# Memory attention feeding a channel mix: nine tokens a partition in head halves, 32x64 tiles for values and token mix, mu by small matmuls, steps placed anew

## The chip, the cores and the metric

One Trainium2 chip, one of its cores. The time is the device time in microseconds of one execution. The kernel before took 222.5 us (median of 9 runs, 221.21 to 223.9); the profiled execution is one of these. A core has a matrix engine (TensorE, PE in the profile; PEld is its weight load), VectorE (DVE), ScalarE (ACT), GpSimd (POOL) and SyncE (SP). Here POOL issues most loads, SP the stores.

## What is computed

q, k, v are (8, 8, 576, 64), phi is (8, 8, 576, 32): batch, head, token, width. All inputs and the output are fp32.

```
a = exp(phi - max); a = a / (sum over the 576 tokens + 1e-9)
k_m, v_m = a^T k, a^T v                     # 32 memory slots a head
e = exp(q k_m^T / 8); attn = e / sum(e)     # over the 32 slots
x = attn v_m                                # heads side by side: (8, 576, 512)

x_prev = x one token later, zero at the first
xk = mu_k * x + (1 - mu_k) * x_prev ;  xr likewise with mu_r
out = sigmoid(xr @ w_r) * (relu(xk @ w_k)^2 @ w_v)     # w_k 512x1024, w_v 1024x512, w_r 512x512
```

The kernels leave the subtraction of the maxima out and do the matrix work in bf16 with fp32 sums.

## The kernel before

The 4608 tokens run through two halves. The attention half works batch by batch (8 batches) and leaves xk and xr transposed, features on the partitions, in two rings `xk_T` and `xr_T` of four batches (2304 columns). The channel mix works in 9 chunks of 512 tokens, whatever batch they belong to. Each chunk has 16 pieces: 8 keys (`key`, L523: four matmuls of 512 columns into one PSUM bank, relu on ScalarE, square on VectorE), 4 gates (`gate`, L537: xr @ w_r, exp; log and exp give the sigmoid for two gates at once) and 4 values (`value`, L556: eight matmuls, the product with the gate on VectorE, the store from SP). In the chunks between the first and the last the order is g0 g1 v0 v1 g2 g3 v2 v3 behind the keys.

The order of all engines is written out by hand in `PLAN`, a list of words: `3:s0+av` is step s0 of batch 3 with its PSUM tiles taken from the pools a and v in turn (a: 3 banks, k: 2, v: 3); `c2:10` is piece 10 of chunk 2 (keys take their bank from k, gates and values from v); `busyN` is N idle matmuls of 512 columns. Each word issues its instructions on all engines; an engine then runs its own in this order. The steps of a batch:

- `load` (`reload`): the loads of batch b+2 on POOL, converted to bf16 on the way for q, k and v. With b+2 over 7 it issues nothing. The buffers are two, so a load waits for the last reader of batch b.
- `exp`: exp of phi; `z` (`esum`): its sum over tokens by matmuls with a column of ones, then the reciprocal rz on VectorE.
- `k`, `v`, `kv` (`ekv`, L268): a^T k and a^T v, 32x64 a head; `nk` (L287), `nv` (L298): times rz, for k twice side by side, for v under a mask into a block-diagonal tile `vbd` of two heads.
- `tk` (L309): transpose of k_m. `q0` to `q3` (`tr_q`, L329): transposes of q on TensorE, copied out by VectorE (in batch 0 half of them by ScalarE). `qx` (`cross_q`, L321): the same by a transposing DMA on SP, for batches 6 and 7.
- `s0`, `s1` (`scores`, L346): for four heads (group c) k_m times q, 32x288 a head and half of the tokens; exp on ScalarE (L350) into `e`.
- `l0` to `l3` (`denom`, L360): sums over the slots by a block of ones, log on ScalarE (L362). `h0z` to `h3z` and `r0z`, `r1z` (`recip`, L367): exp of the negative. `y0` to `y3` and `w0`, `w1` (`weigh`, L374): their product with e on VectorE, into `at`.
- batches 2 to 7: `x0` to `x3` (`values`, L387), copied out by ScalarE (L391), `dd` (`diff`, L400) on VectorE, `k0d`, `k2d`, `r0d`, `r2d` (`mix`, L412) on VectorE.
- batches 0 and 1 mix on TensorE: `nkx`, `nrx` (`norm_mu`, L422) put mu and 1 - mu into the values, `mk0` to `mk3` and `mr0` to `mr3` (`mixed`, L444 and L448) multiply them with the tokens and the tokens before, copied out by ScalarE and VectorE (L453). `mub`, `mum0`, `mum1` (L220, L233) spread mu over the slots; `mu` (L226) puts it on the feature partitions.

Tokens are not kept in their order. Of k, v and phi, partition p holds tokens 4p to 4p+3 of the first 512, and the last 64 tokens sit in a fifth slot of 64 partitions. q has six tokens on each of 96 partitions. The columns of xk are grouped by that slot, `JT = (0, 2, 4, 1, 3, 5)`, in two halves of 288, so that the token before is another group of columns; `store` (L504) puts them back.

```
pss = [ps_tile([128, HALF], F32, "nops") ...]          # values(c, hf): one matmul for each pair of heads
matmul(pss[jj], lhsT=vbd[64 rows of pair jj, c], rhs=at[the same rows, c, half hf])
dst = x[:, 2 * c + jj, half hf]
```

Of the kernel before, what the change touches and what calls it, by code (L numbers as in the profile page):

```python
# [18 lines left out]
    "0:exp 0:z 0:mub 0:mum0 0:mum1 0:k 0:nk 0:busy2 0:tk 0:q0+v 0:q1 0:s0+av 0:l1 0:l0 0:q2+v 0:h0z 0:y0 0:h1z 0:y1",  # L19
    "0:q3+k 0:v 7:load 0:nrx 0:s1+ka 0:l2+v 0:h2z 0:busy1 0:nkx 0:y2 0:l3 0:h3z 0:y3 0:mk0+vv 0:mk1+va 0:busy2",  # L20
    "0:busy2 0:mk3+vv 0:mk2+ak c0:0 c0:1 c0:2 c0:3 c0:4 c0:5 0:mr0+aa 0:mr2+vv c0:6 c0:7 0:mr1+va c0:8 0:mr3+av",
    "1:exp c0:9 c0:10 c0:11 0:load 0:busy1 1:z+v 0:busy1 c0:12 1:k 1:nk 1:q0+k 1:q1+v 0:mu 1:q3 1:tk+k 1:s0+kv",
    "1:q2+v 1:v+v 1:s1+kv 1:l0 1:nrx 1:l1 1:h1z 1:y1 c0:13 1:h0z 1:y0 1:nkx 1:l2 2:exp 1:l3+k 1:load 1:h3z 1:h2z",
    "1:y2 c0:14 c0:15 1:y3 2:z 1:mk1+ka 1:mr1+kv 1:mr3+vv 2:q1 1:mk2+va 1:mr2+ak 2:q0+k 1:mk0+va 2:q2+v 2:q3",
    "1:mk3+ka 1:mr0+vk 2:kv 2:nk c1:0 2:tk+v 2:nv c1:1 c1:2 2:s1+av 2:s0+vv c1:3 c1:4 2:load 2:l3 2:l0 2:l1 c1:5",
    "3:exp c1:6 2:l2+v c1:7 c1:8 3:z 2:r1z c1:9 3:q0 3:q1+v 3:q2 2:w1 c1:10 2:x2+ka 2:r0z 2:x3+ka 3:kv+v 3:nk 2:w0",
    "3:nv c1:11 3:q3+k 3:tk 2:x1+aa 2:x0+kv 2:dd 2:k2d c1:12 3:s0+av 3:s1+aa 3:load 2:k0d c1:13 c1:14 3:l0+k 4:exp",
    "2:r2d c1:15 c2:0 3:l3 3:l1+v 3:r0z c2:1 4:q3 3:w0 3:l2+v c2:2 4:q0 4:q2+v 3:r1z c2:3 4:z c2:4 3:w1 4:kv",
    "3:x1+vv 4:nv 3:x0+va c2:5 3:x3+av 2:r0d 4:nk 3:x2+vv 3:dd c2:6 c2:7 c2:8 5:exp 3:k2d 4:q1 c2:9 4:tk+v c2:10",
    "4:load c2:11 4:s1+ak 6:qx 4:s0+va 3:k0d 5:kv 3:r2d 5:z+v 5:q2+k 4:l3 5:nk 4:l2+k 5:nv c2:12 4:r1z 4:w1 c2:13",  # L30
    "c2:14 c2:15 5:q0+v 4:l1 4:l0+k c3:0 5:q1 6:exp c3:1 3:r0d 5:q3+v c3:2 5:load 6:z+v 4:r0z 5:tk+v 4:w0 c3:3 c3:4",
    "c3:5 4:x3+va 5:s0+va 5:s1+va c3:6 c3:7 c3:8 4:x1+av 4:x2+ka 4:x0+av 6:kv+k 6:nv 6:nk 4:dd 4:k2d c3:9 7:exp",
    "c3:10 c3:11 c3:12 4:k0d 5:l1 4:r0d 5:l0+v 5:r0z 5:w0 5:l3+k 5:l2 7:z+k c3:13 c3:14 6:tk+v c3:15 5:r1z 5:w1",
    "c4:0 c4:1 6:s1+aa 6:s0+av c4:2 5:x2+va 6:load 5:x1+av 7:kv 7:nk c4:3 c4:4 7:qx c4:5 c4:6 c4:7 6:l0+v 4:r2d",
    "5:x0+aa 5:x3+kv 5:dd c4:8 c4:9 6:l3 c4:10 c4:11 7:tk 6:l2+k 5:k2d 6:l1 6:r0z 7:nv 5:k0d c4:12 6:w0 7:s0+aa",
    "7:s1+kv c4:13 6:r1z 6:w1 c4:14 c4:15 c5:0 c5:1 c5:2 c5:3 c5:4 c5:5 5:r2d c5:6 6:x2+va 6:x0+aa c5:7 c5:8",
    "6:x1+ak 5:r0d 6:x3+av c5:9 7:l2+k 6:dd c5:10 6:k0d 7:l0 7:l1+k 7:r0z c5:11 c5:12 c5:13 7:w0 6:k2d 7:l3 c5:14",
    "c5:15 7:r1z c6:0 c6:1 c6:2 c6:3 7:w1 6:r0d c6:4 c6:5 c6:6 c6:7 c6:8 c6:9 6:r2d c6:10 7:x1+av 7:x3+kk 7:x2+aa",
    "c6:11 7:x0+kv 7:dd 7:k0d c6:12 7:k2d c6:13 c6:14 c6:15 c7:0 c7:1 c7:2 c7:3 c7:4 c7:5 c7:6 c7:7 c7:8 c7:9 7:r2d",
    "7:r0d c7:10 c7:11 c7:12 c7:13 c7:14 c7:15 c8:0 c8:1 c8:2 c8:3 c8:4 c8:5 c8:6 c8:7 c8:8 c8:9 c8:10 c8:11 c8:12",  # L40
    "c8:13 c8:14 c8:15",
# [8 lines left out]
NQ = 6  # L50
JT = (0, 2, 4, 1, 3, 5)
NB = 4
TAIL = 512
# [3 lines left out]
def kernel(  # L57
# [13 lines left out]
    nc = tc.nc  # L71
# [9 lines left out]
    NT = S - TAIL  # L81
    HALF = S // 2
    QR = S // NQ
# [10 lines left out]

    NJ = NB + 1
    kvs = [const.tile([128, 2, H, NJ, D], BF16, name=f"kv{i}") for i in range(2)]
    qs = [const.tile([QR, H, NQ, D], BF16, name=f"q{i}") for i in range(2)]
    ems = [const.tile([128, NJ, H, M], BF16, name=f"em{i}") for i in range(2)]
# [5 lines left out]

    def load_phi(b, engs):
        phm = ld.tile([128, H, NB, M], F32, name="phm", tag="phm")
        pht = ld.tile([NT, H, M], F32, name="pht", tag="pht")
        n = H // len(engs)
        for i, eng in enumerate(engs):
            h = slice(i * n, (i + 1) * n)  # L110
            eng.dma_start(
                out=phm[:, h].rearrange("p h j m -> p h (j m)"),
                in_=phi[b, h, 0:TAIL, :].rearrange("h (p j) m -> p h (j m)", j=NB))
        engs[0].dma_start(out=pht, in_=phi[b, :, TAIL:S, :].rearrange("h s m -> s h m"))
        loads[b] = {"phm": phm, "pht": pht}

    def load_rows(dst, src, parts=1):
        n = H // parts
        for i in range(parts):
            h = slice(i * n, (i + 1) * n)  # L120
            nc.gpsimd.dma_start(
                out=dst[:, h, 0:NB, :].rearrange("p h j d -> p h (j d)"),
                in_=src[h, 0:TAIL, :].rearrange("h (p j) d -> p h (j d)", j=NB))
            if i == 0:
                nc.gpsimd.dma_start(out=dst[:NT, :, NB, :],
                                    in_=src[:, TAIL:S, :].rearrange("h s d -> s h d"))

    def load_q(b, parts=1):
        n = H // parts
        for i in range(parts):  # L130
            h = slice(i * n, (i + 1) * n)
            nc.gpsimd.dma_start(  # L132
                out=qs[b % 2][:, h].rearrange("p h j d -> p h (j d)"),
                in_=q[b, h].rearrange("h (p j) d -> p h (j d)", j=NQ))

    def load_batch(b):
        for what in LOADS.get(b, LOADS[None]):
            if what == "phi":
                load_phi(b, [nc.gpsimd])
            elif what == "q":  # L140
                load_q(b)
            else:
                load_rows(kvs[b % 2][:, "kv".index(what)], (k, v)["kv".index(what)][b])

    load_phi(0, [nc.sync, nc.scalar])
    load_rows(kvs[0][:, 0], k[0])
    load_q(0, 2)
    make_identity(nc, identity)
    load_rows(kvs[0][:, 1], v[0], 2)
    nc.vector.memset(zeros, 0.0)  # L150
    for i in range(2):
        nc.vector.memset(kvs[i][64:128, :, :, NB, :].rearrange("p a h d -> p (a h) d"), 0.0)
        nc.vector.memset(ems[i][64:128, NB], 0.0)
# [4 lines left out]
    mu_r = const.tile([64, 2, 2, 2 * D], F32, name="mu_r")  # L158
    sel = const.tile([64, 128], F32, name="sel")
    nc.vector.memset(mu_r, 0.0)  # L160
    nc.vector.memset(sel, 0.0)
    for jj in range(2):
        nc.vector.memset(sel[32 * jj:32 * jj + 1, 64 * jj:64 * jj + 64], 1.0)
        for w, mu in enumerate((moe_mu_k, moe_mu_r)):
            nc.sync.dma_start(out=mu_r[32 * jj:32 * jj + 1, w],
                              in_=mu.rearrange("(c j x) -> j c x", c=2, j=2)[jj:jj + 1])
    mu_bs = []
# [11 lines left out]
    for what in ORDER:  # L179
        if what == "wv":  # L180
            nc.gpsimd.dma_start(out=wv_sb, in_=wv_v)
        elif what == "phi":
            load_phi(1, [nc.gpsimd])
        elif what == "q":
            load_q(1)
        else:
            load_rows(kvs[1][:, "kv".index(what)], (k, v)["kv".index(what)][1])
# [4 lines left out]
    ones = const.tile([128, 1], BF16, name="ones")  # L192
    nc.vector.memset(ones, 1.0)

    maskk = const.tile([128, 2, D], BF16, name="maskk")
    sumh = const.tile([128, 4, M], BF16, name="sumh")
    nc.vector.memset(maskk, 0.0)
    nc.vector.memset(sumh, 0.0)
    for g in range(4):
        r = slice(g * M, (g + 1) * M)  # L200
        nc.vector.memset(maskk[r, g % 2, :], 1.0)
        nc.vector.memset(sumh[r, g, :], 1.0)
    mu1 = const.tile([128, 2 * ND], F32, name="mu1")
    mu_m = const.tile([128, 2, 2, 2, 2 * D], F32, name="mu_m")
# [13 lines left out]
    def load_mu_b():  # L218
        ps = psum.tile([128, 2, 2, 2 * D], F32, name="mub", tag="pk", bufs=2)
        nc.tensor.matmul(ps.rearrange("p w c x -> p (w c x)"), lhsT=sel,  # L220
                         rhs=mu_r.rearrange("p w c x -> p (w c x)"), start=True, stop=True)
        mu_bs.append(ps)
# [5 lines left out]

    def spread_mu(w):

        def go():
            mask = maskk.rearrange("p h d -> p (h d)").unsqueeze(1).to_broadcast([128, 2, 2 * D])
            nc.vector.tensor_mul(mu_m[:, w, 0], mask, mu_bs[0][:, w])  # L233
            nc.vector.tensor_sub(mu_m[:, w, 1], mask, mu_m[:, w, 0])
        return go


    def attention(b):
        st = {}

        def ps_tile(shape, dtype, name):
# [4 lines left out]
            return psum.tile(shape, dtype, name=name, tag=tag, bufs={"at": 3, "pk": 2, "pv": 3}[tag])  # L246
        x0 = b * S % RING
        kv5, em = kvs[b % 2], ems[b % 2]

        def exp_phi():  # L250
            L = loads[b]
            nc.scalar.activation(em[:, 0:NB].rearrange("p j h m -> p h j m"), L["phm"], AF.Exp)  # L252
            nc.scalar.activation(em[:NT, NB], L["pht"], AF.Exp)

        def heads(j, lo, n):
# [352 lines left out]
```

## Time and profile before

| | us |
|---|---|
| median of 9 runs | 222.5 |
| the profiled execution | 221.21 |
| its span in the profile | 219.4 |
| keys L523, TensorE busy | 66.9 |
| values of the channel mix L556, TensorE busy | 65.9 |
| gates L537, TensorE busy | 35.1 |
| TensorE, all | 201.2 |
| ScalarE, all | 162.1 |
| VectorE, all | 139.6 |

The busy time of an engine counts instructions that it runs; overlapping matmuls are counted once. Line numbers are those of the kernel before. A timeline row merges neighbouring instructions of one line and gives the start of the first, the length until the last ends, and how many they are; since matmuls overlap at their ends, the distance to the next row's start is a better measure of what a row costs. A bracket at a row's end tells how long the engine stood idle ahead of it and what released it. TensorE's granted clock is given as full throughout.

### The profile page before, as it was taken

To read this page: it belongs to the slowest core of one execution; us is meant where nothing else is said; L and a number is where in the kernel's file an instruction comes from. 1 tells how busy PE (TensorE), PEld (TensorE's weight loads), DVE (VectorE), ACT (ScalarE), POOL (GpSimd) and SP (SyncE) were. 2 spreads that over 40 slices of the span, in tenths; PEclk is the share of its full clock that TensorE was granted. 3 is DMA by queue.
4 is the path that set the end of the run, shared out by engine and by line. 5 is a ranking of instruction groups with operands and counts; after the bars stand their busy time and mean duration, and the time that the engine had idled before them with its cause. 6 is when DMAs were issued, how large, how long until landed. Compare 5 with 4: busy or idle time off the path is not lost.

```text
span 219.4 us, 4476 instructions
## 1 busy us (share of the span) xinstructions
PE 201.2 (92%) x1700; PEld 99.6 (45%) x1700; DVE 139.6 (64%) x349; ACT 162.1 (74%) x311; POOL 47.9 (22%) x66
## 2 busy tenths in 40 slices
PE   0287999898999999989998999999999999999993
PEld 0134344455455454445444684443444444444442
DVE  5155453479637888996868846867777586725322
ACT  3117578884699898986899789878976985765780
POOL 7573243634444335550100000000000000000000
PEclk9999999999999999999999999999999999999999
DMA  6999999999999999999996370312032033033014
GB/s 144 185 197 207 237 206 227 211 234 248 237 239 198 270 210 257 210 219 267 171 144 185 97 140 0 96 47 52 16 103 75 4 96 96 0 99 96 0 55 136
DMA packets 47477, 32.41 MB, mean 148 GB/s; under 512 B 15584, under 2 KB 41968, under 8 KB 47456
## 3 DMA queue, kind: packets, MB, share of 16 engines
q0 software_dynamic: 35248, 20.91, 63.5%
q1 hardware_dynamic: 11376, 10.63, 19.8%
q10 hardware_dynamic: 832, 0.59, 0.8%
q8 instruction: 13, 0.21, 0.4%
q14 instruction: 8, 0.07, 0.1%
HBM read 38.28 MB, written 9.44 MB: 217 GB/s over the span
## 4 chain that ended last, share of the span: by engine, by line
PE 72%; DMA 11%; DVE 8%; ACT 4%; issue 3%; SPq 1%; POOL 0%; DVEq 0%; POOLq 0%
PE pk L523 26%; PE pv L556 21%; PE pr L537 11%; DMA kv<-in_k_dram 4%; DMA out_dram<-o 4%; PE qtps L329 2%; DMA mu_r<-in_moe_mu_r_dram 2%; PE zps L360 2%; PE nops L387 2%; PE kvps L268 2%; PE mxps L444 1%; PE scps L346 1%; PE idle L215 1%; DVE o L558 1%; PE mub L220 1%
## 5 line engine op out<-in xcount | busy, mean ns | idle before, releaser
L523 PE MATMUL pk<-xkT,wk 128*128 128x512 bf16 (+1 forms) x320 | 66.9, 358 | 0.1
L556 PE MATMUL pv<-wv,sq 128*128 128x512 bf16 (+1 forms) x296 | 65.9, 373 | 0.6 <-DVE rz L281 0.6
L527 ACT ACTIVATE rl<-pk 128x512 bf16<-128x512 f32 x72 | 43.0, 606 | 19.5 <-PE pk L523 19.2
L528 DVE TENSOR_TENSOR sq<-rl 128x512 bf16<-128x512 bf16 x72 | 30.0, 423 | 29.3 <-ACT rl L527 29.0
L523 PEld LDWEIGHTS <-wk 128*128 128x128 bf16 x320 | 30.1, 98 | 29.3 <-issue 2.0
L556 PEld LDWEIGHTS <-sq 128*128 128x128 bf16 x296 | 28.6, 98 | 32.6 <-issue 1.6
L558 DVE TENSOR_TENSOR o<-sg,pv 128x512 f32<-128x512 f32 (+1 forms) x37 | 24.3, 670 | 22.8 <-ACT sg L545 11.8
L537 PE MATMUL pr<-wr,xrT 128*128 128x512 bf16 x144 | 35.1, 380 | 0.6 <-DVE o L558 0.6
L542 ACT ACTIVATE sg<-pr 128x512 f32<-128x512 f32 x36 | 21.5, 608 | 4.9 <-PE pr L537 4.6
L537 PEld LDWEIGHTS <-xrT 128*128 128x128 bf16 x144 | 13.2, 98 | 16.3 <-issue 2.3
L544 ACT ACTIVATE sg<-sg 128x1024 f32<-128x1024 f32 x18 | 19.0, 1057 | 0.6
L545 ACT ACTIVATE sg<-sg 128x1024 f32<-128x1024 f32 x18 | 19.0, 1057 | 0.6
L391 ACT CAST x<-nops 128x288 bf16<-128x288 f32 x48 | 15.8, 433 | 1.4 <-PE nops L387 1.4
L412 DVE TENSOR_SCALAR mu_d<-diff,mu 128x576 bf16<-128x576 bf16 x48 | 16.2, 380 | 0.1
L374 DVE TENSOR_TENSOR atn<-e,lz 128x576 bf16<-128x576 bf16 (+1 forms) x20 | 12.6, 633 | 4.2 <-ACT lz L367 4.2
L362 ACT ACTIVATE lz<-zps 128x288 f32<-128x288 f32 x32 | 11.7, 406 | 3.1 <-PE zps L360 3.0
L350 ACT ACTIVATE e<-scps 128x288 bf16<-128x288 f32 x32 | 10.8, 429 | 2.8 <-PE scps L346 2.8
L333 DVE COPY qT<-qtps 128x576 bf16<-128x576 bf16 x22 | 9.5, 450 | 4.4 <-PE qtps L329 4.4
L367 ACT ACTIVATE lz<-lz 128x576 f32<-128x576 f32 (+1 forms) x20 | 11.4, 584 | 0.3
L252 ACT ACTIVATE em<-phm 128x1024 bf16<-128x1024 f32 x8 | 8.4, 1056 | 2.3 <-DMA phm<-in_phi_dram 2.3
L329 PE MATMUL qtps<-identity,q 96*128 96x96 bf16 x144 | 10.0, 219 | 0.0
L132 POOL DMA_DIRECT2D q<-in_q_dram x9 | 6.8, 760 | 13.3 <-PE qtps L329 6.4
(71 smaller groups left out, 187.9 us busy)
## 6 DMA issues: line engine op xcount, KB each, us to landing
out_dram<-o SPq DMA_DIRECT2D x23, 192.0 KB, 3.9
kv<-in_k_dram POOLq DMA_DIRECT2D x8, 512.0 KB, 11.7
q<-in_q_dram POOLq DMA_DIRECT2D x7, 576.0 KB, 13.5
phm<-in_phi_dram POOLq DMA_DIRECT2D x7, 512.0 KB, 12.8
kv<-in_v_dram POOLq DMA_DIRECT2D x7, 512.0 KB, 14.2
out_dram<-o SPq DMA_DIRECT2D x23, 128.0 KB, 2.6
out_dram<-o SPq DMA_DIRECT2D x23, 64.0 KB, 3.0
wk<-in_moe_w_k_dram POOLq DMA_DIRECT2D x2, 512.0 KB, 11.5
```

The costliest lines, as they stand in the source:

```text
L329: nc.tensor.matmul(ps[:, i, j], rhs=identity[:QR, :QR], is_transpose=True, lhsT=qs[b % 2][:, 2 * pr + i, 2 * j:2 * j + 2, :].rearrange("p ...
L391: nc.scalar.copy(st["x"][:, 2 * c + jj, sl], pss[jj])
L412: nc.vector.tensor_scalar_mul(t[:, i], st["d"][:, pr + i, :], mu1[:, o:o + 1])
L523: nc.tensor.matmul(pk[:, lo:hi], lhsT=wk_sb[:, di, fi * 128:(fi + 1) * 128], rhs=xk_T[:, di, c0:c0 + hi - lo], start=(di == 0), stop=(di = ...
L527: nc.scalar.activation(rl, pk, AF.Relu)
L528: nc.vector.tensor_mul(st["sq"][:, fi, :], rl, rl)
L537: nc.tensor.matmul(pr, lhsT=xr_T[:, di, c0:c0 + 128], rhs=wr_sb[:, di, :], start=(di == 0), stop=(di == ND - 1))
L542: nc.scalar.activation(sg[:, ts % 2], pr, AF.Exp, scale=-1.0)
L544: nc.scalar.activation(sg, sg, AF.Ln, bias=1.0)
L545: nc.scalar.activation(sg, sg, AF.Exp, scale=-1.0)
L556: nc.tensor.matmul(pv[:, cols], lhsT=st["sq"][:, fi, ts * 128:(ts + 1) * 128], rhs=wv_sb[:, fi, cols], start=(fi == 0), stop=(fi == NF - 1))
L558: nc.vector.tensor_mul(o[:, cols], st[ts // 2][:, ts % 2, cols], pv[:, cols])
```

## The change

Data. `NQ`, `NB`, `TAIL` go; for q, k, v and phi alike partition p holds nine tokens 9p to 9p+8, of heads 0 to 3 on partitions 0 to 63 and of heads 4 to 7 on partitions 64 to 127. A load is two DMAs of 64 partitions (three for phi, whose second half swaps neighbouring heads). The halves of a batch's columns are 320 and 256, in the order `JT = (0, 2, 4, 6, 8, 1, 3, 5, 7)`. The memsets of unused partitions go.

```
+        engs[0].dma_start(out=ph[ROWS[0]]..., in_=rows(phi[b], 0))
+        for i in range(2):
+            engs[1].dma_start(out=dst[:, i], in_=src[:, 1 - i])
+        for hg in range(2):
+            nc.gpsimd.dma_start(out=dst[ROWS[hg]]..., in_=rows(src, hg))
...
-            nc.scalar.activation(em[:, 0:NB]..., L["phm"], AF.Exp)
-            nc.scalar.activation(em[:NT, NB], L["pht"], AF.Exp)
+            nc.scalar.activation(em.rearrange("p j h m -> p h j m"), loads[b], AF.Exp)
```

Matmuls of the attention half. a^T k and a^T v contract 64 partitions instead of 128, in nine slots instead of five: 72 matmuls instead of 40, in two PSUM tiles instead of one. The sums take 9 instead of 10, with two columns. The q transposes are 36 of 64 columns in two steps instead of 24 of 96 in four; `qx` issues two DMAs.

```
-                    for h in range(H):
-                        c, g = divmod(h, 4)
-                        nc.tensor.matmul(kvps[g * M:(g + 1) * M, c], lhsT=em[:, j, h, :],
-                                         rhs=kv5[:, parts, h, j, :], ...
+                    for g in range(HH):
+                        for c in range(2):
+                            nc.tensor.matmul(kvps[c][g * M:(g + 1) * M], lhsT=em[ROWS[c], j, g, :],
+                                             rhs=kv5[ROWS[c], parts, g ^ c, j, :], ...
...
+                for n in range(NJ):
+                    n0 = 2 * (NJ * i + n)
+                    for hg in range(2):
+                        r = ROWS[hg]
+                        nc.tensor.matmul(pss[hg][:, n], rhs=identity[r, r], is_transpose=True,
+                                         lhsT=qs[b % 2][r, n0:n0 + 2, :]..., ...
```

The scores read both q steps for either group (`n = 9 * (g ^ c) + j`). Values and token mix no longer use a block-diagonal tile: `norm_v` is two plain products of 64 columns, `norm_mu` two instructions instead of four, and each head is a matmul of its own, 32 rows by 64 columns, four to a call:

```
+        def head_tiles(jj, pss, src, lo, hi, cols=slice(0, None), **flags):
+            for c in range(2):
+                for g in (2 * jj, 2 * jj + 1):
+                    r, i = slice(g * M, (g + 1) * M), (g + c) % 2
+                    nc.tensor.matmul(pss[c][i * D:(i + 1) * D, cols], lhsT=src[r, c], rhs=st["at"][r, c, lo:hi], ...
...
-        def values(c, hf):
+        def values(jj, hf):
+                head_tiles(jj, pss, st["vb"], sl.start, sl.stop, start=True, stop=True)
+                for c in range(2):
+                    nc.scalar.copy(st["x"][:, 2 * c + jj, sl], pss[c])
...
+        before = [[(QR, 5 * QR, 5 * QR), (1, QR, 4 * QR)], [(5 * QR, S, 0)]]
-        def mixed(w, c, hf):
+        def mixed(w, jj, hf):
+                head_tiles(jj, pss, vm[:, 0], lo, hi, start=True, stop=False)
+                for n, (c0, c1, p0) in enumerate(before[hf]):
+                    head_tiles(jj, pss, vm[:, 1], p0, p0 + c1 - c0, slice(c0 - lo, c1 - lo), ...
```

Mu. `mu_r` is read by two DMAs instead of four onto four partitions; `mub` is two fp32 matmuls, each a group's 128 columns with a 4-row selector made from the identity, and two VectorE instructions; `mum0` and `mum1` go.

```
+        for c in range(2):
+            nc.tensor.matmul(ps[:, :, c], lhsT=sel[:, c]..., rhs=mu_r[:, :, c], start=True, stop=True, ...)
+        nc.vector.tensor_copy(mu_m[:, :, 0], ps)
+        nc.vector.tensor_scalar(mu_m[:, :, 1], ps, -1.0, 1.0, op0=AL.mult, op1=AL.add)
```

The output tiles `o` are four instead of three. `PLAN` is written anew throughout; its start up to chunk 1's first key, the two words around each `qx`, and its end:

```
+    "0:busy2 0:busy2 0:exp 0:z 0:k+aa 0:nk 0:tk 0:mub 0:q0+ka 0:q1+av 0:s0+ak 0:s1+va 0:l0+v 0:l1 0:v+vk 0:nrx",
+    "0:h1z 0:y1 0:h0z 0:nkx 0:l2+k 0:y0 0:l3 0:h3z 0:y3 0:mu+k 0:h2z 0:y2 0:mk3+ka 0:mk0+ak 0:mk1+vv 0:mk2+va",
+    "0:busy2 0:busy2 0:mr0+aa c0:0 c0:1 0:load 6:load c0:2 c0:3 c0:4 c0:5 0:mr3+av 0:mr1+aa 0:mr2+vv c0:6 c0:7",
+    "1:exp c0:8 c0:9 c0:10 1:z c0:11 1:k+va 1:nk 1:tk+k 1:q1+ak 1:q0+va c0:12 1:s0+vv 1:v+aa 1:nkx 1:nrx 1:load",
+    "1:s1+av c0:13 1:l1 1:l0 1:l2+v 1:l3+k 1:h1z 1:y1 1:h2z 1:y2 1:h0z 1:y0 1:h3z 1:y3 c0:14 c0:15 2:exp 1:mk2+ak",
+    "1:mk0+aa 1:mr2+vv 1:mr3+av 1:mr0+ka 1:mk3+va 1:mk1+va 1:mr1+kv 2:z 2:q0+vk 2:q1+av c1:0 2:kv+va 2:nk 2:nv c1:1",
...
c2:6 4:load 6:qx 5:exp c2:7
...
c3:10 7:qx c3:11
...
c8:13 c8:14 c8:15 0:busy2
```

## The prediction

> **What bounds the kernel now.** I read the page's busy shares first, then the shares in slices, then TensorE's timeline, then the timeline of the GpSimd queue.
>
> ```profile
> PE 201.2 (92%) x1700; PEld 99.6 (45%) x1700; DVE 139.6 (64%) x349; ACT 162.1 (74%) x311; POOL 47.9 (22%) x66
> ...
> PE   0287999898999999989998999999999999999993
> ...
> DMA  6999999999999999999996370312032033033014
> ```
>
> TensorE (PE) is the bound, but not everywhere: the first five slices (to 27 us) are thin, slices 8 to 10 (38 to 55 us) have holes, and from there it is full to the last slice. The transfers are dense for the first 120 us, yet TensorE is full while they are, so after the start they don't end last. So there are three stages, cut at the first key matmul (L523) of chunk 0 and of chunk 1:
>
> ```profile
> 10.00 2.07 PE L220 MATMUL mub<-mu_r,sel 64*128 64x512 f32 x2 [2.81 <-DMA mu_r<-in_moe_mu_r_dram]
> 12.00 0.73 PE L268 MATMUL kvps<-kv,em 128*32 128x64 bf16 x40
> ...
> 23.10 1.89 PE L215 MATMUL idle<-zeros 128*128 128x512 bf16 x4
> ...
> 25.52 5.51 PE L523 MATMUL pk<-xkT,wk 128*128 128x512 bf16 x24
> ...
> 40.36 0.49 PE L268 MATMUL kvps<-kv,em 128*32 128x64 bf16 x40
> 40.78 0.68 PE L329 MATMUL qtps<-identity,q 96*128 96x96 bf16 x12
> ...
> 43.16 0.32 PE L346 MATMUL scps<-qT,kmT 64*32 64x288 bf16 x8 [1.07 <-DVE kmT L312]
> ...
> 55.90 1.04 PE L523 MATMUL pk<-xkT,wk 128*128 128x512 bf16 x4
> ```
>
> Columns: start, length, engine, line, tiles, operand shapes, count, wait. Stage 1 ends at 25.52, stage 2 lasts 55.90 - 25.52 = 30.4 us, stage 3 lasts 219.4 - 55.9 = 163.5 us. Stage 3's prices come from starts that follow each other:
>
> ```profile
> 64.79 0.39 PE L278 MATMUL zps<-ones,em 128*128 128x1 bf16 x10
> 65.04 1.02 PE L537 MATMUL pr<-wr,xrT 128*128 128x512 bf16 x4
> 65.90 0.93 PE L329 MATMUL qtps<-identity,q 96*128 96x96 bf16 x18
> 66.67 1.89 PE L556 MATMUL pv<-wv,sq 128*128 128x512 bf16 x8
> 68.49 0.42 PE L387 MATMUL nops<-atn,vbd 64*128 64x288 bf16 x4
> 68.84 0.74 PE L268 MATMUL kvps<-kv,em 128*32 128x128 bf16 x40
> 69.52 1.90 PE L556 MATMUL pv<-wv,sq 128*128 128x512 bf16 x8
> ```
>
> and from the chain of work that ended last (start, length, what):
>
> ```profile
> 14.65 0.97 PE qtps L329 x12
> ...
> 58.78 0.37 PE scps L346 x16
> ...
> 66.83 1.73 PE pv L556 x8
> ```
>
> A 512-column matmul takes 1.73/8 = 0.216 us, so 0.42 ns a column. The q transposes take 0.77/18 = 43 ns each, the size of their 96 columns. Four value matmuls take 0.35 us: two pairs side by side are 2 x 0.12, and 0.11 are over. Forty kv matmuls take 0.68: ten rounds of four at 0.053 are 0.53, and 0.15 over. I book the excess as a change of tile shape, about 0.065 us each. Ten ones-matmuls with 128-column weights take 0.25, so 23 to 25 ns is the pitch of such a weight load.
>
> **Stage 1, to the first key.** Before, the k/v product waited behind the fp32 mu matmul (to 12.0). Now it comes ahead of it. Its data sets it, as the GpSimd queue shows, where the ninth load waits for the first to land and the twelfth for the fourth:
>
> ```profile
> 10.28 0.74 POOL L176 DMA_DIRECT2D wk<-in_moe_w_k_dram  x1 [2.47 <-DMA kv<-in_k_dram]
> ...
> 13.55 0.89 POOL L111 DMA_DIRECT2D phm<-in_phi_dram  x1 [0.58 <-DMA q<-in_q_dram]
> ```
>
> So k lands at 10.2, q at 13.5. The same bytes move in rows of 2304 B instead of 1024 and 256 B; I keep the landings, with 2 us earlier as the good bound. From 10.3: 72 small matmuls 0.73 to 1.2 us (12.00's row for 40, times 72/40), 11.4; kbd 0.6 and k's transpose 0.55, 12.8; mu on half the columns, 2.07/2, 13.8. It hides in the wait for q. The 36 transposes of 64 columns at 81 ns x 64/96 (12 took 0.97 here, at about half the later speed), 1.9 us, 15.8; last copy 0.64, 16.4; scores 0.6, 17.0; then ScalarE alone sets the pace: four exp (0.71 a pair), four log and four reciprocals (0.71 and 0.78 a pair), 4.4 us, 21.4; the last weighing on VectorE 0.46, 21.9. Before it ended at 23.6. But a mix step now multiplies both head groups and shifts across the halves, so each needs all four weighed quarters; before, mk0 and mk1 needed two. Four mix steps at half clock are 2 x 1151 columns x 0.83 ns = 1.9 us; then four idle matmuls at 0.45 (row 23.10) and one receptance step. First key: 25.9, that is 0.4 later, but with that step's 0.3 us done. Bounds 23.5 (earlier data, the steps side by side) and 27.5 (the 72 at 23 ns, q no earlier).
>
> **Stage 2, chunk 0 with batch 1.** Work in it before: 80 matmuls of 512 columns 17.25; 12 mix steps 4.1; q transposes of two batches 2.06; two half kv products 0.84 and batch 2's whole 0.67; scores, log sums, transposes, sums 1.8; idle 0.5: 27.2, so 3.2 us of waits (40.8 to 43.2 is the largest: kbd, three q copies and kmT in a row on VectorE, with scores behind). After: 17.25; mix 3 + 8 steps 2.6; transposes 2 x 0.9; two half kv 0.4 to 0.66 each, 1.1; the rest 1.7: 24.4. Waits: k's transpose stands right behind kv and norm, so TensorE stands still for kbd, 0.8; the eight mix steps are evacuated by two engines, 8 x 0.43 = 3.4 us beside some 2 us of matmuls, which leaves 1.5. Sum 26.7. So -3.7, of which 0.67 is batch 2's kv moved into stage 3. Queued behind the 0.8 us wait are only q's transposes, which nobody needs before the scores. If the old waits come back, 24.4 + 5 = 29.4 is the bad end; 25 the good one.
>
> **Stage 3.** Values: 24 pairs at 0.12 = 2.9 us become 96 matmuls in 12 visits of eight, all on different tiles. If the eight run side by side: 256 and 320 columns, 0.24 a batch, 1.45 in all, -1.45. If only four do, 0; if the two row groups that share a bank go in turn and nothing else overlaps, +2.9. I take side by side: scores (64x32, eight at once) cost 16 in 0.37, two rounds and the excess. q: three batches x (36 x 23 ns = 0.83 against 1.03) = -0.6, bounds -1.6 and 0. kv: 72 on eight tiles are 9 x 0.053 = 0.48; the pitch shown at 40.36 is at most 0.42/40 = 10 ns, or 7.3 without the excess, so 0.53 against 0.53; and one visit more, +0.53. Shape changes go from 41 to 47, +0.4. Sums nine for ten, -0.1. Together -1.2: 162.3. ScalarE's exp of phi loses its second instruction (1.05 + 0.40 become about 1.15 by the slope of 0.88 ns a column between its 512 and 1024 rows); norm of v and mixes shrink on VectorE; both are off the bound here. Loads: nine transfers a batch for seven, about 7 us of GpSimd issue, on a queue that is 22% busy and mostly waits; uncovered, it would cost the 1 us of extra issue. The load steps moved ahead (0:load from behind gate 3 to behind key 1) issue into a queue that waits for landings anyway. On SP the two transposes of q become four half ones; the stores behind them held VectorE's output at 118.4, which cost TensorE 0.59; a fourth output buffer covers more: batch 6's transpose now waits on SP for the q load issued just before it, with chunk 2's four output tiles stored behind it, and the fifth tile is asked for at chunk 3's first value, at least 20 us of matmuls on. The load lands 13.5 us (median) after its issue, the transposes take 3.4 to 6.1. I book 0; each us by which that is missed would stand on TensorE. The closing idle matmuls lie beside the last store.
>
> The Trainium skill, "TensorEngine Tiling (Array Packing)", Gotcha 1: PSUM Pressure, holds that different row tiles can't use one PSUM bank at the same time; values and mixes now put two row groups into one bank, on different partitions, which no row of before shows. By that rule the eight would go in two rounds and the time would be 1.45 us more than mine. "TensorE: Matmul & The Clock Gate", Wait — 56ns, not 53.3ns?, sets a floor of about 25 ns from start to start for small matmuls; the row at 40.36 shows 10 at most, so the measurement decides against it; by the page the kv products alone would cost about 10 us more.
>
> **Sum.** 25.9 + 26.7 + 162.3 = 214.9 against 219.4: -4.5. The profiled execution took 221.2, its span and 1.8 around it, and was the lowest of nine; applied to the median of 222.5 this is 218.0.
>
> **Rivals.**
> 1. *More gain, 214.3.* Data lands 2 us earlier because there are a third as many rows in k (512 for 1536), and mixes run eight tiles wide (another 1 to 2 us). For it: more than half of all packets are under 2 KB. Against it: wk's 2048-byte rows moved no faster (about 2.5 us for 1 MB read, as v's 1024-byte rows, 1.3 us for 0.5 MB).
> 2. *The waits come back, 221.3.* Stage 2 at 29.4 and the first key 0.6 later: 218.0 + 3.3. For it: scores of either group now need both q copies, mixes all four quarters. Against it: a chunk's values lie between those steps.
> 3. *Small tiles are paced by issue, 227: slower.* One mechanism: each small matmul with its own weights costs a fixed pitch, whatever runs beside it. kv alone has 432 in stage 3 and 144 uncovered in stage 2. At 23 ns, the pitch of 128-column loads, (23 - 7.3) x 576 = 9.0 us. It makes the kernel 0.5% slower than before from (4.5 + 1.1) / 576 + 7.3 = 17 ns. Against it: 40 in 0.42 us, whose weights are just as narrow; for it: those are four tiles of all rows, not eight of half.
>
> **Chances.** Mine 0.38, rival 1 0.20, rival 2 0.17 (half of it inside the bound), rival 3 and kin 0.25. A measurement here can tell 0.5%, 1.1 us. Faster 0.38 + 0.20 + 0.08 = 0.66, same 0.09, slower 0.25. My own case spans 215.5 to 220.5; with the good bounds of stage 1 and part of rival 3, 214 to 225.
>
> **What would show it.** First key near 25.9 us, chunk 1's first key near 52.6; a kv visit of 72 in 0.55 to 0.7 us (rival 3: over 1.2); eight value matmuls to the next start in 0.25 us, against 0.37 or more if they don't pair; an 18-transpose group near 0.45; no wait on TensorE over 1 us behind 55 us. I am wrong if kv visits pass 1.2 us, if the first key comes after 27.5, or if stage 3 holds new waits for VectorE's diff and mix.

## The result and the profile after

The changed kernel takes 220.81 us (median of 21 runs, 218.61 to 224.22), the kernel before in the same sessions 222.81 us (median of 63). The ratio is 0.9895, with a 95% interval of 0.9875 to 0.9915: 1.05% faster, where 2.0% were forecast. The profiled execution took 223.5 us, its span 221.7; it lies 1.2% above the median. TensorE ran at half clock for some time behind two waits, which are shown below, and its mean granted clock is 0.977. Ratios, here and below, leave out each kernel's slow runs (over 1.5% above its fastest); medians take all.

The page of the changed kernel, busy shares and slices:

```profile
PE 200.8 (91%) x2215; PEld 98.9 (45%) x2215; DVE 132.3 (60%) x332; ACT 159.7 (72%) x303; POOL 46.2 (21%) x79
...
PE   3397998996999999999954999999999999999993
...
PEclk9999999997999999999996799999999999999999
DMA  6999999999999999999998930242044044044025
```

TensorE's busy time is what it was (201.2), though it runs 515 more matmuls. The thin start has become shorter (the third slice is already a 9, with transposes and scores). But there is a new hole in slices 21 and 22 (111 to 122 us), with a lower clock in it and behind it, and a smaller one in slice 10 (50 to 55 us).

TensorE's timeline of the changed kernel, the rows of the three stages (columns as in the prediction):

```profile
8.66 0.40 PE L248 MATMUL zps<-ones,em 128*128 128x2 bf16 x9 [5.58 <-ACT em L227]
8.99 0.81 PE L239 MATMUL kvps<-kv,em 64*32 64x64 bf16 x72
...
11.88 1.14 PE L304 MATMUL qtps<-identity,q 64*128 64x64 bf16 x36
13.16 1.14 PE L323 MATMUL scps<-qT,kmT 64*32 64x320 bf16 x16
...
18.36 1.66 PE L271 MATMUL mxps<-atn,vm 32*64 32x256 bf16 x38 [0.69 <-DVE atn L351]
...
22.26 5.35 PE L483 MATMUL pk<-xkT,wk 128*128 128x512 bf16 x24
...
48.97 1.04 PE L483 MATMUL pk<-xkT,wk 128*128 128x512 bf16 x4
...
52.04 0.79 PE L239 MATMUL kvps<-kv,em 64*32 64x128 bf16 x71 [1.88 <-DMA kv<-in_v_dram]
52.76 3.56 PE L483 MATMUL pk<-xkT,wk 128*128 128x512 bf16 x8
...
118.86 0.38 PE L248 MATMUL zps<-ones,em 128*128 128x2 bf16 x9 [5.14 <-DVE o L518]
119.69 0.68 PE L323 MATMUL scps<-qT,kmT 64*32 64x320 bf16 x16 [0.45 <-DVE kmT L284]
120.30 1.89 PE L497 MATMUL pr<-wr,xrT 128*128 128x512 bf16 x4
121.99 4.82 PE L516 MATMUL pv<-wv,sq 128*128 128x512 bf16 x16
```

| stage | before | forecast | after, profiled |
|---|---|---|---|
| 1, to chunk 0's first key | 25.5 | 25.9 | 22.3 |
| 2, to chunk 1's first key | 30.4 | 26.7 | 26.7 |
| 3, the rest | 163.5 | 162.3 | 172.7 |
| span | 219.4 | 214.9 | 221.7 |

Against the forecast, stage 1 is 3.6 us shorter, stage 2 falls on it, and stage 3 is 10.4 us longer. The last six rows tell of what. TensorE waits 1.88 us for batch 2's v, 5.14 for VectorE's output tile, 0.45 for k's transpose: 7.5 us. Behind the waits the rows are slow: eight keys take 3.56 us (1.90 in other rows of eight), and from start to start the scores take 0.61 for 0.37, four gates 1.69 for 0.87, sixteen values 4.75 for 3.55, together 3.9 us more. Less the 0.59 us which the kernel before had lost at its store and the forecast kept, that is 10.8 us, so the 10.4 are accounted for in this execution; the median of all runs lies 2.7 us under it.

What stopped TensorE for 5.14 us stands in VectorE's timeline of the changed kernel:

```profile
118.12 1.31 DVE L518 TENSOR_TENSOR o<-sg,pv 128x512 f32<-128x512 f32 x2 [8.65 <-DMA out_dram<-o]
```

and what that store waited for in the chain of the work that ended last, of the changed kernel (start, length, what):

```profile
98.84 8.07 SPq L294
...
107.00 0.54 SPq L464
...
107.59 10.41 DMA out_dram<-o
...
118.12 0.58 DVE o L518
```

and the same place in the chain of the kernel before:

```profile
108.89 9.40 DMA out_dram<-o
118.41 0.70 DVE o L558
119.14 1.02 PE pr L537 x4
```

SP's queue first runs the two transposing DMAs of batch 6 (L294), then issues a store, which lands 10.41 us later and frees the output tile. It frees it at 118.1 us, where the kernel before had it at 118.4: TensorE comes to this point earlier, and the store does not. The time won ahead of it is waited out there: TensorE goes on at 118.86 us, in the kernel before at 119.14.

### The profile page after: what moved, and what is told of

It is laid out like the page before. It is cut to its first block, busy times and chain, and to the rows that moved or that the text cites. A ratio compares the mean times of both kernels' runs of the same rounds, so it can differ in the third digit from the quotient of the medians.

```text
span 221.7 us, 5494 instructions
## 1 busy us (share of the span) xinstructions
PE 200.8 (91%) x2215; PEld 98.9 (45%) x2215; DVE 132.3 (60%) x332; ACT 159.7 (72%) x303; POOL 46.2 (21%) x79
## 4 chain that ended last, share of the span: by engine, by line
PE 65%; DMA 26%; SPq 4%; issue 2%; DVE 1%; POOL 1%; POOLq 0%; DVEq 0%
PE pv L516 24%; PE pk L483 23%; PE pr L497 12%; DMA wv<-in_moe_w_v_dram 8%; DMA kv<-in_v_dram 5%; DMA out_dram<-o 5%; DMA ph<-in_phi_dram 4%; SPq L294 4%; DMA kv<-in_k_dram 3%; PE kvps L239 2%; PE nops L271 1%; PE zps L337 1%; PE scps L323 1%; POOL kv L116 1%; DVE o L518 1%
## 5 line engine op out<-in xcount | busy, mean ns | idle before, releaser
L516 PE MATMUL pv<-wv,sq 128*128 128x512 bf16 (+1 forms) x296 | 67.1, 378 | 0.0
L363 ACT CAST x<-nops 128x256 bf16<-128x256 f32 (+1 forms) x48 | 15.7, 422 | 2.8 <-PE nops L271 2.7
L327 ACT ACTIVATE e<-scps 128x320 bf16<-128x320 f32 (+1 forms) x32 | 10.8, 436 | 6.6 <-PE scps L323 6.6
L116 POOL DMA_DIRECT2D kv<-in_k_dram x16 | 10.0, 629 | 19.1 <-PE kvps L239 5.2
L351 DVE TENSOR_TENSOR atn<-e,lz 128x576 bf16<-128x576 bf16 (+2 forms) x20 | 12.4, 632 | 1.4 <-ACT lz L344 1.3
L116 POOL DMA_DIRECT2D q<-in_q_dram x16 | 9.8, 614 | 16.2 <-PE qtps L304 4.0
L339 ACT ACTIVATE lz<-zps 128x320 f32<-128x320 f32 (+1 forms) x32 | 12.0, 429 | 1.6 <-PE zps L337 1.5
L116 POOL DMA_DIRECT2D kv<-in_v_dram x16 | 9.8, 614 | 14.7 <-DMA wv<-in_moe_w_v_dram 4.5
L248 PE MATMUL zps<-ones,em 128*128 128x2 bf16 x72 | 3.0, 164 | 10.7 <-ACT em L227 5.6
L227 ACT ACTIVATE em<-ph 128x1152 bf16<-128x1152 f32 x8 | 9.3, 1163 | 4.0 <-DMA ph<-in_phi_dram 4.0
```

What stands on the lines that cost most here:

```text
L116: nc.gpsimd.dma_start(out=dst[ROWS[hg]].rearrange("p h j d -> p h (j d)"), in_=rows(src, hg))
L363: nc.scalar.copy(st["x"][:, 2 * c + jj, sl], pss[c])
L516: nc.tensor.matmul(pv[:, cols], lhsT=st["sq"][:, fi, ts * 128:(ts + 1) * 128], rhs=wv_sb[:, fi, cols], start=(fi == 0), stop=(fi == NF - 1))
```

## Experiments

Medians in us; ratio to the kernel before, run on the same chip, with its 95% interval.

| | time | ratio |
|---|---|---|
| the change | 220.81 | 0.9895 [0.9875, 0.9915] |
| E1, q of batches 6 and 7 on TensorE | 216.82 | 0.9732 [0.9684, 0.9780] |
| E2, one transposing DMA for two | 223.47 | 0.9898 [0.9844, 0.9953] |
| E3, eight output tiles | 219.0 (215.73 to 220.89) | none given, runs too far apart |
| E4, three output tiles | 228.13 | 1.0236 [1.0156, 1.0317] |
| E5, transposing DMAs later | 218.82 | 0.9786 [0.9699, 0.9872] |
| E6, E1 with batch 2's products later | 216.57 | 0.9702 [0.9624, 0.9781] |
| E7a, E7b, batch 0's loads split | 219.87, 222.06 (one run each) | |
| E9, the kernel before, q on TensorE | 228.86 | 1.0262 [1.0204, 1.0321] |
| E11, E6 with values in four tiles | 217.08 | 0.9763 [0.9718, 0.9807] |

**E1: without the transposing DMAs.** The q of batches 6 and 7 is transposed on TensorE, as that of the others.

```
-    4:load 6:qx 5:exp        ...  c3:10 7:qx c3:11 6:tk
+    4:load 5:exp             ...  c3:10 c3:11 6:q0+aa 6:q1+vv 6:tk
-    c4:10 5:k2d c4:11
+    c4:10 7:q0+aa 7:q1+vv 5:k2d c4:11
```

> The changed kernel with the q transposes of batches 6 and 7 on TensorE (steps q0 and q1 in chunk 3 and chunk 4) in place of the two transposing DMAs each. Theory 1, the transposing DMAs on SP hold the stores, VectorE runs out of output tiles, TensorE stops for 5.1 us near 114 us and then runs at half clock for some 4 us: no such stop, 2 x 0.64 us more transposes, so 5.1 + 2 - 1.3 = about 5 to 6 us under the changed kernel, 215 to 216 us. Rival, any store is late there because loads are dense: the stop remains and the time is 1 us longer than the changed kernel, about 222.

216.82 us, 4 us under the change's median; the 5 to 6 that were expected start from its profiled execution, which is a long one. Its TensorE timeline, where the hole was:

```profile
107.62 3.62 PE L516 MATMUL pv<-wv,sq 128*128 128x512 bf16 x16
111.17 0.70 PE L304 MATMUL qtps<-identity,q 64*128 64x64 bf16 x36
...
112.38 0.64 PE L337 MATMUL zps<-e,sumh 128*128 128x320 bf16 x2 [0.16 <-DVE qT L308]
...
113.72 0.37 PE L248 MATMUL zps<-ones,em 128*128 128x2 bf16 x9
114.02 0.44 PE L323 MATMUL scps<-qT,kmT 64*32 64x320 bf16 x16
```

The sums that waited until 118.86 now start at 113.72, although 36 transposes were added ahead of them (0.63 us). The list of issues between 90 and 112 us (issues, KB each, median us to landing) shows the other side. The changed kernel:

```profile
out_dram<-o SPq DMA_DIRECT2D x7, 128.0 KB, 10.4
...
qT<-q SPq DMA_TRANSPOSE x2, 16.7
```

and E1:

```profile
out_dram<-o SPq DMA_DIRECT2D x8, 128.0 KB, 4.0
```

Stores of the same size, beside loads of the same kind, land in 4.0 instead of 10.4 us when no transposing DMA is ahead of them on their queue.

**E2: is it that there are two of them?** One DMA over all 128 partitions for both halves; the tile's layout and its readers follow.

```
-            for hg in range(2):
-                nc.sync.dma_start_transpose(out=q_tile()[:, hg], in_=qs[b % 2][ROWS[hg]]...)
+            nc.sync.dma_start_transpose(out=q_tile()..., in_=qs[b % 2]...)
```

> The changed kernel with one transposing DMA of 128 partitions a batch instead of two of 64 (qT laid out pair, head group, token). If cutting the transpose in halves is what makes it slow (qT landed 15.4 to 18.0 us after its issue, 6.6 before): landing 6 to 8 us, the SP queue free some 8 us earlier, no stop on VectorE over 1 us, about 216 us. If the earlier place (loads of batches 6 and 7 in flight) makes it slow: landing stays over 12 us, about 220.

Its ratio is that of the change: no gain (the 223.47 us in the table is the median of all its ten runs). SP's timeline of E2:

```profile
97.86 8.96 SPq L293 DMA_TRANSPOSE qT<-q  x1
106.93 13.98 SPq L463 DMA_DIRECT2D out_dram<-o  x10
```

One holds the queue for 8.96 us, the two of the change for 10.68, the one of the kernel before 6.06. The store behind it frees its tile at 119.09, and TensorE waits 5.83 us. That there are two is not the cause. The transpose lands 19.7 us after its issue, so the expectation's second branch, the earlier place beside the loads, is the one that fits.

**E3 and E4: more and fewer output tiles.**

```
-                o = work.tile([128, Dm], F32, name="o", tag="o", bufs=4)
+                o = work.tile([128, Dm], F32, name="o", tag="o", bufs=8)     # E4: bufs=3
```

> The changed kernel with eight output tiles instead of four. Theory 1 (the stop is VectorE without an output tile): VectorE's wait for a store, 8.65 us, is gone although the stores stay late; 5 to 7 us under the changed kernel, 214 to 216. If the stop comes from qT landing late for batch 6's scores instead: no change, 220 to 221.

> The changed kernel with three output tiles, as before the change. Theory 1: VectorE stops one value earlier, so TensorE stops about 2 us longer (a value of 1.73 us): 222 to 224. If the number of tiles doesn't bear on the stop: 220 to 221.

With eight, VectorE waits for no store any more, as theory 1 has it. The median of the four runs, 219.0 us, is 1.8 less than the change's and above the 214 to 216 expected, but they spread from 215.73 to 220.89, so what part of E1's gain this is stays open. TensorE's timeline of E3 shows a stop that E1 does not have:

```profile
112.56 0.37 PE L248 MATMUL zps<-ones,em 128*128 128x2 bf16 x9
114.80 0.59 PE L323 MATMUL scps<-qT,kmT 64*32 64x320 bf16 x16 [1.88 <-DVE atn L351]
115.33 1.89 PE L497 MATMUL pr<-wr,xrT 128*128 128x512 bf16 x4
117.01 4.29 PE L516 MATMUL pv<-wv,sq 128*128 128x512 bf16 x16
```

The sums come at 112.56, 6.3 us earlier than in the change, but the scores behind them wait 1.88 us, and the next four gates take 1.68 instead of 0.87. The bracket names VectorE, whose product ended at 114.7; but the second transposing DMA, issued at 99.48, lands 15.2 us later, at 114.7 too, and the scores read what it writes. So more output tiles cure the stores, not the late transpose. With three tiles the stop comes sooner and is longest, in TensorE's timeline of E4:

```profile
110.88 0.64 PE L304 MATMUL qtps<-identity,q 64*128 64x64 bf16 x17 [13.00 <-DVE o L518]
111.45 4.97 PE L483 MATMUL pk<-xkT,wk 128*128 128x512 bf16 x12
```

228.13 us, 2.4% slower than before, and more than the 222 to 224 expected: the value that now finds no tile is chunk 2's last, for which VectorE stands idle from 95.4 us, 14 us ahead of chunk 3's first. So the fourth tile covers some 8 us of this stop (13.0 less 5.1), and without it the change would have made the kernel slower.

**E5: the transposing DMAs later.** `6:qx` goes behind c2:15, `7:qx` behind c3:15, so that chunk 2's stores are ahead of the first.

> The changed kernel with 6:qx moved from behind c2:6 to behind c2:15 and 7:qx from behind c3:10 to behind c3:15, nothing else. Theory 1a, the place in SP's queue is what hurts (the q load isn't there yet, and chunk 2's four stores stand behind the transposes): the four stores go out ahead, VectorE finds an output tile at chunk 3's first value, the 5.1 us stop of TensorE is gone, 215.5 to 217. Rival 1b, the transposes themselves are too slow wherever they stand (15 to 18 us to land): the stop moves to the next values of chunk 3 and the time stays at 219 to 221.

218.82 us, between the two expectations. The store wait is gone, and the next one stands in its place, in TensorE's timeline of E5:

```profile
115.39 0.44 PE L323 MATMUL scps<-qT,kmT 64*32 64x320 bf16 x16 [3.45 <-DMA qT<-q]
```

Batch 6's scores now wait for the transpose itself, which lands 13.6 us after its issue. Of the two places on SP that were tried, neither serves both the stores and the scores.

**E6: batch 2's products later, on top of E1.** `2:kv 2:nk 2:nv` go from behind c1:0 behind c1:2, `2:tk` behind c1:3, `3:exp` with it.

> The first experiment's kernel (q of batches 6 and 7 on TensorE) with 2:kv, 2:nk and 2:nv moved behind c1:2, two keys later, and 2:tk behind c1:3. If batch 2's v load, landing at 52.0 us, is the only thing that holds TensorE there: its wait of 1.4 us shrinks to under 0.3 and the time falls by about 1 us, to 215.5. If the wait only moves (to k's transpose or the scores): no change, 216.8.

216.57 us, the best of all versions, but only 0.25 under E1, which these runs don't tell apart. The wait of 1.37 us for v is gone; new small ones came, 0.37 for k's transpose and 0.5 for q's.

**E7: does row length set when batch 0's data lands?** Its k and q come by four DMAs each: E7a two heads each (rows of 2304 bytes), E7b five and four tokens (rows of 1280 and 1024).

```
+                h = slice(2 * i, 2 * i + 2)                       # E7a
+                nc.gpsimd.dma_start(out=dst[ROWS[hg], h]..., in_=rows(src, hg)[:, h])
...
+                j = (slice(0, 5), slice(5, 9))[i]                 # E7b
+                nc.gpsimd.dma_start(out=dst[ROWS[hg], :, j]..., in_=rows(src, hg)[:, :, 64 * j.start:64 * j.stop])
```

> The changed kernel; batch 0's k and q are loaded by four DMAs instead of two, two heads each: rows stay 2304 B, 512 rows a tensor. Base for the next one: first kv matmul 1 to 1.3 us later than in the changed kernel (8.99 us) if the two added issues of 0.6 us set it, otherwise at 9.0.

> The changed kernel; batch 0's k and q are loaded by four DMAs, five and four tokens of all heads each: the same bytes and issues as with heads split, in 1024 rows of 1280 and 1024 B a tensor. If the length of rows is what let k and q land 1.4 to 1.9 us earlier than before the change: first kv matmul at least 0.7 us later than with heads split. If bytes alone set the landing: the same within 0.3 us, and the earlier landing has another cause.

The 72 products start at 8.24 us in E7a and at 8.34 in E7b, some 0.7 earlier than in the change, which neither expectation had. In all three the products stand right behind the sums, and these wait for the exp of phi, so it is not k that ends last, and the start of the products says little about rows. The landings of k do: 5.3 us after the issue in E7a, 5.2 to 5.5 in E7b (medians, one run each), so a factor of about two in row length shows no difference to speak of. Rows of 256 bytes, as the kernel before had for its last 64 tokens, were not tried.

**E9: would E1's edit have helped the kernel before?** In it `6:qx` and `7:qx` give way to `6:q0+v 6:q1 6:q2+v 6:q3` behind c3:14 and `7:q0+v 7:q1 7:q2+v 7:q3` behind c4:11.

> The kernel before, with batch 6's and 7's q transposed on TensorE (three words of six behind c3:14, three behind c4:11) in place of the two transposing DMAs. If the queue's stop stood in the kernel before too and only its slower TensorE hid it, little is to be won: it lost 0.59 us there, and 2 x 1.03 us of transposes are added, so 222 to 224.5 us, ratio 1.00 to 1.01. If the gain of the first experiment had nothing to do with the change and would come in either kernel, 218 to 219 us, ratio near 0.98.

228.86 us, 2.6% slower: longer, as expected, but by more than the 222 to 224.5 allow. Its TensorE timeline:

```profile
122.78 1.19 PE L329 MATMUL qtps<-identity,q 96*128 96x96 bf16 x24
125.60 0.27 PE L309 MATMUL ktps<-identity,kbd 128*128 128x128 bf16 x2 [1.64 <-DVE o L558]
125.97 3.04 PE L556 MATMUL pv<-wv,sq 128*128 128x512 bf16 x7
```

The transposes take 2 x 1.19 us; a new wait of 1.64 follows, then seven values take 2.83 us to the next row instead of 1.5. These are 5.3 us, where 6.2 lie between the medians and 8.2 between the two profiled spans; of the latter, 1.8 stand ahead of the edit (chunk 0's first key comes at 27.31 us instead of 25.52). The copies of the transposes and k's transpose share VectorE and the PSUM pools there, so the place that I gave the words may have its part in this. E9 shows that E1's edit, in these places, wins nothing in the kernel before; it is no clean price of the transposes, and whether another place would have won something stays open.

**E11: what makes the values cheap?** E6, with the eight value matmuls of a visit taken from two steps that use the same four tiles.

```
-    2:x1+ak 2:x3+kv ... 2:x2+ka 2:x0+vk        # likewise batches 3 to 7
+    2:x0+ak 2:x1+kv ... 2:x2+ka 2:x3+vk
```

> The best version so far (q of batches 6 and 7 on TensorE, batch 2's norms later), with the values' eight matmuls of a step taken from chunks 0 and 1, then 2 and 3, so that the eight sit in four tiles only and not in eight. If eight side by side is what makes them cheap: about 0.12 us more for each of the 16 steps, of which some 12 lie on the path: +1.4 us, 218.0 us against 216.6. If rows that share a bank go in turn anyway, no difference: 216.6 us, eight values 0.25 us as now.

The time moved by 0.5 us of the medians, by 1.4 of the ratios, whose intervals overlap; the rows decide. TensorE's timeline of E6:

```profile
66.82 0.34 PE L271 MATMUL nops<-atn,vb 32*64 32x320 bf16 x8
67.09 1.90 PE L497 MATMUL pr<-wr,xrT 128*128 128x512 bf16 x8
```

and of E11:

```profile
66.16 0.44 PE L271 MATMUL nops<-atn,vb 32*64 32x320 bf16 x8
66.53 1.90 PE L497 MATMUL pr<-wr,xrT 128*128 128x512 bf16 x8
```

In E6 a visit has eight matmuls of 320 columns, 0.27 us to the next start, or of 256 columns, 0.25; in E11 it has four of each in the same four tiles, and every visit takes 0.37. So the eight of the change run side by side, two row groups into one bank among them; in two rounds they would take about E11's time.

## The prediction, point by point

**Direction and range right, size wrong: the step that failed is "I book 0" for SP's queue.** From the issue of batch 6's second q load (88.2 us) it took 13.5 us for the load, 3.4 to 6.1 for the transposes and nothing for the store, against "at least 20 us of matmuls". Measured are 8 us until SP goes on (96.2), 10.7 for the transposes, and 10.4 for the landing of the store behind them: 118.0. The fifth tile is asked for 21.3 us behind that issue, at 109.5. So the margin was read well. Load and transposes together took 18.7 us where 16.9 to 19.6 were booked, by luck: the load's part was 5.5 us shorter than booked, the transposes 4.6 longer than the most that was booked. What was left out is the store's landing behind them, which is all of the 8.65 us by which the tile is late. It could have been read from the chain of the kernel before, which has it: 9.40 us, in the lines shown above. The prediction said that a miss would stand on TensorE microsecond for microsecond; of VectorE's 8.65 us, 5.14 stand there. Its sign "no wait on TensorE over 1 us behind 55 us" fails with them. That the direction came out all the same owes something to luck too: stage 1 was missed by 3.6 us the other way.

**The miss cost more than its length**, since the clock fell behind it: scores, gates and values took 2.3 us more there than elsewhere. Nothing in the prediction priced that.

**A second wait was not listed:** batch 2's v, 1.88 us, at chunk 1's start. The prediction had moved batch 2's products into stage 3 with their busy time (0.67) and without asking whether their data is there. With stage 1 shorter than forecast, it is late. E6, which takes this wait out of E1, is 0.25 us faster, so it is worth little where the clock stays up.

**Stage 1 was mis-sized by 3.6 us, for the better.** The products started at 8.99 instead of 10.3. Product and transposes at the start cost 0.8 and 1.28 instead of 1.1 and 1.9, since I scaled the 40 products and 12 transposes of the kernel before by their number and columns. And the scores began right behind the transposes, without the copy of 0.64 that I put between them. These are 2.9 of the 3.6 us; the sum itself ran 0.25 high (11.4 and the 1.15 for kbd and k's transpose are 12.55, not 12.8). In part that is rival 1's outcome (data 2 us earlier), but why is not shown: E7 speaks against the row length that I gave for it, as far as it was tried, and why the start moved stays open beyond that.

**Stage 2 came out at 26.7 us as forecast, by two misses that cancel.** TensorE's waits in it are 0.48 us for k's norm, 0.24 for q's load and 0.24 for a copy of the mixes, 1.0 where 0.8 and 1.5 were booked; the rows take 25.7 us where the sum has 24.4. Rival 2's waits did not come back. Chunk 1's first key lies 3.6 us ahead of the forecast's 52.6 because of stage 1.

**The prices of stage 3 held.** TensorE's timeline of the changed kernel:

```profile
63.66 0.70 PE L304 MATMUL qtps<-identity,q 64*128 64x64 bf16 x36
64.30 1.90 PE L516 MATMUL pv<-wv,sq 128*128 128x512 bf16 x8
66.13 0.32 PE L271 MATMUL nops<-atn,vb 32*64 32x256 bf16 x8
66.37 0.80 PE L239 MATMUL kvps<-kv,em 64*32 64x128 bf16 x72
67.11 1.90 PE L516 MATMUL pv<-wv,sq 128*128 128x512 bf16 x8
```

From start to start, 72 products take 0.74 us, just above the 0.55 to 0.7 that the prediction asked for, and far from rival 3's 1.2: that is 10 ns each, so these small tiles are not paced at 23 ns. Eight values take 0.24 (forecast 0.25), the 36 transposes 0.64, less than the 0.83 booked. The Trainium skill, "TensorEngine Tiling (Array Packing)", Gotcha 1: PSUM Pressure, which holds that row tiles can't use one bank at the same time, is not borne out for tiles on different partitions of the bank: by its rule the eight would go in two rounds, as E11's do in 0.37 us (forced there by the tiles, not by the bank), and the change has 0.24 to 0.27.

**Where the forecast's time is found.** With the transposing DMAs gone, E1's span is 215.6 us and E6's 214.7, against 214.9 in the sum. This is no proof of the sum: E1's stage 1 is 3.0 shorter than forecast and its stage 3 is 166.0, 3.7 longer, of which 1.3 are the added transposes and 2.5 two waits (1.4 for v, 1.1 for VectorE's output).

## What to carry to other kernels

Where a change makes the bounding engine faster, ask of each transfer that frees a buffer whether it keeps its place in absolute time; the kernel before already shows it, as a short wait at the end of a long landing in the chain. Count a store's landing into the chain that ends in its buffer, with the price that it has in that place (10.4 us here, where the median of all stores of the kernel is 2.4). And try to keep a slow transfer that waits for a load off the queue that stores results, even if the bounding engine has to do its work: that won 4 us in the changed kernel, though in the kernel before, in the places tried, it lost 6 (E9).

## What the runs showed of the hardware

- A short stop of TensorE can halve its speed behind it. After waits of 1.88 us (the change and E3), 5.14 and 13.0 us (E4, twelve keys in 4.97 us), the next rows ran at about half speed; after 1.37 us (E1, the same place) eight keys took the usual time. Length alone does not decide it: 1.64 us were enough in E9 (seven values in 2.83 us, clock 0.66 from 125 to 130 us), while 1.66 us left E3's keys at full speed, in its TensorE timeline:

```profile
51.84 0.79 PE L239 MATMUL kvps<-kv,em 64*32 64x128 bf16 x71 [1.66 <-DMA kv<-in_v_dram]
52.56 1.90 PE L483 MATMUL pk<-xkT,wk 128*128 128x512 bf16 x8
```

  The granted clock agrees: it is 1.00 ahead of the wait for v and 0.83 in the ten microseconds that hold it, and 0.76 and 0.56 around the end of the wait of 5.14, in the windows of the changed kernel (window, TensorE's busy time and the other engines', clock, DMA share, GB/s):

```profile
40.00:50.00 10.00, 9.76 (x157) 5.23 (x156) 8.09 (x22) 6.62 (x19) 4.35 (x8) 1.00 1.18 242
50.00:60.00 10.00, 8.11 (x115) 3.60 (x115) 3.83 (x12) 4.84 (x10) 5.02 (x9) 0.83 1.17 247
...
115.00:120.00 5.00, 0.69 (x25) 0.44 (x24) 1.88 (x5) 0.50 (x1) 0.00 (x0) 0.76 0.70 221
120.00:125.00 5.00, 5.00 (x29) 1.78 (x14) 4.90 (x11) 4.03 (x7) 0.00 (x0) 0.56 1.12 154
```

  In windows of half a microsecond the clock is half from 52.7 to 56.2 us and from 117.6 to 124.4, that is for 3.4 and 6.8 us; behind E3's 1.88 and E9's 1.64 it is half for 3.4 us as well. So a stop of under 2 us cost another 1.3 (E9's values) to 1.7 us (the change's keys).
  The Trainium skill, "TensorE: Matmul & The Clock Gate", What's actually happening, has the clock fall after an idle window of about 3.4 us; here 1.64 and 1.88 us of standing still were enough.
- Transposing DMAs from one on-chip buffer to another held their queue far longer beside loads than without: the change's two for batch 6 held it for 10.7 us with loads beside them, its two for batch 7 for 3.5 behind the last loads. E2's single ones landed 19.7 us after the issue with loads beside them, 5.3 with none.
